# FFT convolution of one 224x224 image with a 7x7 kernel: the order of the first copies, and which pixel transforms precede the first round

## The chip, the cores and the metric

The kernel runs on one core of a Trainium2 chip. The core has five engines that run side by side: TensorE (PE, matrix products; its weight loads are listed as PEld), VectorE (DVE), ScalarE (ACT), GpSimd (POOL) and SyncE (SP), which here only issues DMA transfers. Data comes from HBM into SBUF (128 partitions); products land in PSUM (8 banks), from where VectorE or ScalarE evict them. The metric is the device time of one launch in microseconds, the median of several runs. Lower is better.

## The reference

A circular convolution over a 224x224 image with 96 input and 96 output channels, 7x7 taps, written as a product of spectra. Inputs are bfloat16, the spectra are float32, and the result is rounded to bfloat16.

```python
# x: (1, 224, 224, 96), w: (7, 7, 96, 96), both bfloat16
def reference(x, w):
    B, H, W, C = x.shape
    K = w.shape[0]
    wp = jnp.pad(w, ((0, H - K), (0, W - K), (0, 0), (0, 0)))
    Xf = jnp.fft.rfft2(x.astype(jnp.float32), axes=(1, 2))
    Wf = jnp.fft.rfft2(wp.astype(jnp.float32), axes=(0, 1))
    Yf = jnp.einsum('bhwi,hwio->bhwo', Xf, Wf)
    return jnp.fft.irfft2(Yf, s=(H, W), axes=(1, 2)).astype(jnp.bfloat16)
```

## The kernel before, in words

**What it computes.** Rows are transformed, columns are not. The 224 rows are cut into 8 blocks of 28 output rows; each block with its 6 rows of overlap is taken to 17 "slots" s = 0..16 by a matrix `Fm` (a DFT of length 32 and two extra real values). Slots 0 and 16 hold two real values each, the other 15 a complex one, which is multiplied with three real products (parts 0, 1, 2). Along a row the 7 taps are applied directly, on even and odd pixels apart, with 10 tap matrices per slot and part (`NTAP`, 7 taps and 3 sums). Per slot the channels are contracted on TensorE by matmuls of 96 columns with the transformed weights `WF` (`b_round`). The results `yf` go to a scratch in HBM, are loaded again, and a matrix `G` takes them back to rows.

**Tiles.** The image is worked in 7 tiles of 32 columns (t = 0..6). A tile's pixels come in two halves of 112 rows and 6 overlap rows (`jg` = 0, 1). Tile 0 lies in `x0_bufs`, tile 1 in `xn_bufs`; tile 0 also needs 6 columns from the right edge of the image, the halo (`xh_bufs`).

**Pixel transforms.** `f_jobs(t, part)` transforms the pixels of tile 0, 1 or 2 for a range of slots: `SH2 = (0, 8, 13, 17)` makes part 0 slots 0 to 7, part 1 slots 8 to 12, part 2 slots 13 to 16. A job is 8 or 16 matmuls (weights are one pixel column, moving data is `Fm`, 64, 40 or 32 columns wide for the three parts) into a PSUM bank, and one eviction to `xf`. Each part and half has 32 matmuls. The halo is done by `a_bank`. `jit(t, g)` then builds on VectorE the differences and sums `J` of a group of three slots, which the rounds read.

**Weights.** The 49 tap matrices of 96x96 lie with taps on partitions. A first copy stands on partitions 30 to 78 of `wqx` (`W1 = 30`), a second, shifted by 48 output channels, on 79 to 127. Each copy is one transfer of 48 rows (`load_w`) and two of the last row (`load_last`). The unused places of `wqx` are set to zero by ScalarE (`zero_a`) and one memset. `wide_jobs` (24 jobs of four matmuls, eviction to `WF`) makes the weights of slots 0 to 4 from the first copy alone. `prep_jobs(gi)` makes those of slots 5 to 16, in four groups of three slots, from both copies. `diff(s)` makes part 2 from parts 0 and 1.

**What sets the order.** Every engine runs its instructions in the order written: the class `_Ordered` (line 91) chains them. An eviction goes to VectorE or ScalarE by a running cost of each (`load`, line 132). All loads are issued by SP, one after the other; SP waits for an earlier transfer's landing when it needs that transfer's semaphore again. The head (lines 203 to 223) issues the loads and starts 14 dummy matmuls; GpSimd, VectorE and ScalarE build the factors `Em`, the transform `Fm` and the zero fills; `build_g` (line 339) computes `G` on GpSimd, with one Sin on ScalarE and a last product in `g_fin`. Then follow (lines 759 to 778) the pixel jobs of half 0, the wide jobs, with halo, half 1 of part 0 and `jit(0, 0)` among them, and dummy matmuls in between.

**Rounds.** After the head, tiles 0 and 1 run as one sequence of rounds r = 0..20 (line 819): tile 0 does slot r, and from r = 4 on tile 1 does slot r - 4. Each round has two places for other work, in mid round and at its end, numbered k = 2r and 2r + 1. `add(a, b, jobs)` spreads a list of jobs over the places a to b - 1; the lists run at each place in the order in which they were added, the `prep_jobs` ahead of the pixel jobs. The first group of `prep_jobs` begins at place 4, the middle of round 2. Tiles 2 to 6 follow, tile by tile.

Of the kernel before, what the change touches and what calls it, by code (L numbers as in the profile page):

```python
# [47 lines left out]
FILL = 3  # L48
FEV = 4
WMID = 14  # L50
JIT0 = 20
W1 = 30
ZA = 1000
# [13 lines left out]
def kernel(  # L67
# [134 lines left out]

    load_x(0, 0)
    load_last(K1 - 1, 0)
    load_w(W1, 0, PW - 1, 0)
# [33 lines left out]
    pi_t = ftile([128, 1])  # L239
    VE.memset(pi_t[:], math.pi)  # L240
    dmy = ftile([128, 1])
    SE.activation(out=dmy[:], in_=pi_t[:], func=ACTF.Sin, bias=0.0, scale=0.0)
# [7 lines left out]

    nrj = ftile([EP, JG]); pw_i = ftile([EP, 1]); aa = ftile([EP, NS, 2]); phf = ftile([EP, NS, 2]); phe = ftile([EP, NS, 2])
# [16 lines left out]
    VE.scalar_tensor_tensor(out=tap[:], in0=ha[:], scalar=-float(PW), in1=pw_i[:], op0=ALU.mult, op1=ALU.add)  # L268
    floor_div(VE, thp[:], tap[:], KT)
# [9 lines left out]
    SE.activation(out=qq[:], in_=qq[:], func=ACTF.Sin, bias=pi_t[:], scale=-2.0 * math.pi / Q)  # L279
    zero_a(W1, ZA, ZB)  # L280

    GE.memset(mf[:], 1.0)
# [10 lines left out]
    iota(twc[:], [[1, KT]])  # L293
    twp = ftile([EP, 1]); mk = ftile([EP, NTAP]); mk2 = ftile([EP, 2, NTAP])
    th7 = ftile([EP, 1])
    GE.tensor_single_scalar(out=th7[:], in_=thp[:], scalar=-float(KT), op=ALU.mult)
    GE.tensor_tensor(out=twp[:], in0=th7[:], in1=tap[:], op=ALU.add)
    GE.tensor_scalar(out=mk[:, 0:KT], in0=twc[:], scalar1=twp[:, 0:1], scalar2=None, op0=ALU.is_equal)
    GE.tensor_tensor(out=mk[:, KT:NTAP], in0=mk[:, 0:6:2], in1=mk[:, 1:6:2], op=ALU.add)
    VE.scalar_tensor_tensor(out=hm[:, 0:1], in0=hb[:], scalar=-2.0, in1=ha[:], op0=ALU.mult, op1=ALU.add)  # L300
    VE.scalar_tensor_tensor(out=hm[:, 1:2], in0=pw_i[:], scalar=float(PW), in1=hm[:, 0:1], op0=ALU.is_ge, op1=ALU.subtract)
    for h in range(2):
        GE.tensor_scalar(out=mk2[:, h], in0=mk[:], scalar1=hm[:, h:h + 1], scalar2=None, op0=ALU.mult)
    for xb in xh_bufs:
        GE.memset(xb[:, PAD * C:], 0.0)
    for xb in xn_bufs:
        GE.memset(xb[:, XW:], 0.0)

    VE.tensor_tensor(out=Fm.rearrange("p r s j -> p j s r"), in0=qq[0:R, 0:JG],
                     in1=mf.rearrange("p j (s r) -> p j s r", r=2), op=ALU.mult)  # L310
    qe = qq[:, JG]
    pe3 = ftile([EP, NSLOT])
    VE.memset(wz[0:W1, ZB:WE // 2], 0.0)
# [8 lines left out]
    def factors(h0, h1, out_ap, in_ap):  # L322
# [7 lines left out]
        else:  # L330
# [5 lines left out]
            pe3[:, 5:14].rearrange("p (s r) -> p s r", r=3)[:, :, 0:2])  # L336
    factors(0, 2, Em[:, :, NW0:], pe3[:, NW0:])
    factors(1, 2, Em[:, 1, 0:NW0], pe3[:, 0:NW0])

    def build_g(nj):  # L340
        PG = nj * FR

# [9 lines left out]
        p = ftile([PG, 1]); sp = ftile([PG, 1]); rm = ftile([PG, 1]); jp = ftile([PG, 1]); rr = ftile([PG, 1]); z = ftile([PG, 1])  # L352
        iota(p[:], [[0, 1]], cm=1)
        mod_g(rm[:], p[:], jp[:], FR)
        mod_g(rr[:], rm[:], sp[:], 2)
        GE.tensor_single_scalar(out=z[:], in_=sp[:], scalar=0.0, op=ALU.is_equal)
        zr = ftile([PG, 1]); ag = ftile([PG, 1]); pg = ftile([PG, 1]); amp = ftile([PG, 1]); pgt = ftile([PG, 1])
        GE.tensor_tensor(out=zr[:], in0=z[:], in1=rr[:], op=ALU.mult)
        GE.tensor_scalar(out=ag[:], in0=zr[:], scalar1=LC / 2.0, scalar2=sp[:, 0:1], op0=ALU.mult, op1=ALU.add)
        en = ftile([PG, 1]); ne = ftile([PG, 1]); tg = ftile([PG, 1])  # L360
        GE.tensor_single_scalar(out=en[:], in_=sp[:], scalar=NS - 1.0, op=ALU.is_equal)
        GE.tensor_scalar(out=ne[:], in0=en[:], scalar1=-1.0, scalar2=1.0, op0=ALU.mult, op1=ALU.add)
        GE.tensor_scalar(out=ag[:], in0=ag[:], scalar1=2.0, scalar2=ne[:, 0:1], op0=ALU.mult, op1=ALU.mult)
        GE.tensor_tensor(out=pgt[:], in0=rr[:], in1=zr[:], op=ALU.subtract)
        GE.tensor_tensor(out=pgt[:], in0=pgt[:], in1=ne[:], op=ALU.mult)
        GE.tensor_scalar(out=pg[:], in0=pgt[:], scalar1=LC / 2.0, scalar2=LC / 2.0, op0=ALU.mult, op1=ALU.add)
        GE.tensor_scalar(out=amp[:], in0=z[:], scalar1=-1.0 / LC, scalar2=2.0 / LC, op0=ALU.mult, op1=ALU.add)
        GE.tensor_tensor(out=amp[:], in0=amp[:], in1=ne[:], op=ALU.mult)
        GE.tensor_tensor(out=amp[:], in0=amp[:], in1=en[:], op=ALU.add)
        GE.tensor_scalar(out=tg[:], in0=rr[:], scalar1=B - 1.0, scalar2=PAD - 1.0, op0=ALU.mult, op1=ALU.add)  # L370
        GE.tensor_tensor(out=tg[:], in0=tg[:], in1=en[:], op=ALU.mult)
        GE.tensor_single_scalar(out=jp[:], in_=jp[:], scalar=2.0 * B, op=ALU.mult)
        GE.tensor_tensor(out=tg[:], in0=tg[:], in1=jp[:], op=ALU.add)
        nm = ftile([PG, nj, B]); jc = ftile([PG, nj, B]); msk = ftile([PG, nj, B]); fl = ftile([PG, nj, B]); th = ftile([PG, nj, B])
        iota(nm[:], [[0, nj], [1, B]], base=PAD - 1)
        iota(jc[:], [[2 * B, nj], [0, B]])
        GE.tensor_scalar(out=msk[:], in0=nm[:], scalar1=en[:, 0:1], scalar2=None, op0=ALU.mult)
        GE.tensor_tensor(out=msk[:], in0=msk[:], in1=jc[:], op=ALU.add)
        GE.tensor_scalar(out=msk[:], in0=msk[:], scalar1=tg[:, 0:1], scalar2=amp[:, 0:1], op0=ALU.is_equal, op1=ALU.mult)
        GE.tensor_scalar(out=nm[:], in0=nm[:], scalar1=ag[:, 0:1], scalar2=pg[:, 0:1], op0=ALU.mult, op1=ALU.add)  # L380
        mod_g(th[:], nm[:], fl[:], Q)

        def fin():
            SE.activation(out=th[:], in_=th[:], func=ACTF.Sin, bias=pi_t[0:PG, :], scale=-2.0 * math.pi / Q)
            GE.tensor_tensor(out=G.rearrange("p (j m) -> p j m", j=nj), in0=th[:], in1=msk[:], op=ALU.mult)
# [140 lines left out]
    def jit(t, g):  # L526
# [10 lines left out]
        def sub(o, a, b, op, cost):  # L537
            def f():
# [7 lines left out]
        dpl = bass.AP(x1.tensor, x1.offset - NJ, [pd, [NJ, 2], rd, sd, qd])  # L546
        return [
            sub(Jb[:, 0:4, 0:n].rearrange("c (k r) s q -> c k r s q", r=2), dpl,
                x0.unsqueeze(1).to_broadcast([C, 2, 2, n, PP]), ALU.subtract, 4 * PP * n),
# [211 lines left out]
    for p in range(3):  # L761
        for f in fj[p][0]:
            f()
    warm(FILL)
    for i, f in enumerate(wide_jobs()):
        if i == WMID:
            for jg in range(2):
                for g in a_bank(0, xf0, xh_bufs[jg], 0, 3, jg, 0):
                    g()
            for g in fj[0][1]:  # L770
                g()
        f()
        if i == JIT0:
            for g in jit(0, 0):
                g()
        if i % FEV == FEV - 1:
            warm(1)
    g_fin()
    stmp_cm.__exit__(None, None, None)
    yf_pool = ctx.enter_context(tc.tile_pool(name="yf", bufs=YBUF))  # L780
    tv_pool = ctx.enter_context(tc.tile_pool(name="tv", bufs=2))
# [193 lines left out]
```

## Time and profile before

| | us |
|---|---|
| median of 3 runs (lowest, highest) | 271.03 (269.06, 271.15) |
| the profiled execution | 269.31 |
| its span on the core | 267.5 |

| stretch of the span | length, us | PE busy, us | what runs on TensorE |
|---|---|---|---|
| 0 to 6.73 | 6.73 | 5.36 | 14 dummy matmuls |
| 6.73 to 10.67 | 3.94 | 3.34 | 96 pixel matmuls of half 0, 3 dummies |
| 10.67 to 20.73 | 10.06 | 9.12 | wide jobs, halo, half 1 of part 0, dummies |
| 20.73 to 27.20 | 6.47 | 5.13 | rounds 0, 1 and the start of 2 |
| 27.20 to 37.70 | 10.50 | 10.47 | rounds 2 to 4 |
| 37.70 to 60 | 22.30 | 21.52 | rounds |
| 60 to 230 | 170.00 | 168.83 | rounds and tiles 2 to 6 |
| 230 to 267.4 | 37.40 | 31.28 | last tile's end and output |

Times inside the span are counted from its start. Busy times are what the profile records; matmuls overlap, so the spacing of their starts tells what one costs. The rest of a run's time, 269.31 - 267.5 = 1.8 us, lies around the span.

### The profile page before, as it was taken

Reading aid. Unit: us, or ns where it says so; the run is one execution under the profiler, and the core shown is the slowest. Engines: PE = TensorE matmul, PEld = TensorE weight load, DVE = VectorE, ACT = ScalarE, POOL = GpSimd, SP = SyncE. Lnnn points to the kernel's source line nnn. Section 1 sums busy time; section 2 is a strip of 40 time slices with the busy share of each in tenths; the row PEclk is TensorE's granted clock in tenths of the full one; section 3 lists DMA queues with packets and bytes.
Section 4 is the critical chain, followed back from the end, with each engine's and each line's share of the span. In section 5 each row is a group of like instructions: output and inputs, shape, how many; then the busy total and the mean of one; then the engine's idle time right before and its main releaser. Section 6 shows DMA issues by size and latency. Waiting matters only on the chain. (4 is left out here: it accounts for less than half of the span.)

```text
span 267.5 us, 12139 instructions
## 1 busy us (share of the span) xinstructions
PE 255.1 (95%) x5128; PEld 235.7 (88%) x5128; DVE 216.2 (81%) x465; ACT 197.6 (74%) x485; POOL 97.7 (37%) x152
## 2 busy tenths in 40 slices
PE   8897999999999999999999999999999999999983
PEld 2787999999998999999999998989999889879861
DVE  7997699889899788778887888778888789978523
ACT  8796978497964578998988789886988864187123
POOL 7771324364558344222222322233123323422100
PEclk9999999999999999999999999999999999999998
DMA  8994102711111697987876486979678443887845
GB/s 197 230 251 76 48 2 67 245 45 48 47 48 49 192 258 159 294 238 223 272 195 188 117 235 221 253 216 341 235 152 242 169 128 125 204 250 182 259 107 191
DMA packets 46690, 46.78 MB, mean 175 GB/s; under 512 B 35292, under 2 KB 38056, under 8 KB 46540
## 3 DMA queue, kind: packets, MB, share of 16 engines
q1 hardware_dynamic: 44348, 43.95, 59.6%
q10 hardware_dynamic: 2288, 2.06, 2.6%
q8 instruction: 40, 0.66, 1.1%
q14 instruction: 14, 0.11, 0.2%
HBM read 24.66 MB, written 21.33 MB: 172 GB/s over the span
## 5 line engine op out<-in xcount | busy, mean ns | idle before, releaser
L101 PE MATMUL pb<-WF,J 96*128 96x96 bf16 x2821 | 162.9, 206 | 1.7 <-DVE J L101 1.3
L101 PEld LDWEIGHTS <-J 96*128 96x128 bf16 x2821 | 138.0, 98 | 12.3 <-issue 3.5
L101 POOL TENSOR_TENSOR yf<-v,u 128x384 bf16<-128x384 f32 x79 | 81.3, 1040 | 145.7 <-issue 84.6
L101 ACT CAST xf<-pb 96x408 bf16<-96x408 f32 (+3 forms) x145 | 67.3, 486 | 7.6 <-PE pb L101 3.8
L101 PE MATMUL pb<-WF,xf 96*128 96x96 bf16 x952 | 60.0, 206 | 0.9 <-ACT WF L101 0.9
L101 DVE TENSOR_TENSOR J<-xf 96x1824 bf16<-96x1824 bf16 (+1 forms) x84 | 56.9, 716 | 0.0
L101 PEld LDWEIGHTS <-xf 96*128 96x128 bf16 x952 | 47.2, 98 | 1.3 <-issue 1.2
L101 PE MATMUL pb<-Fm,xn 118*128 118x136 bf16 (+3 forms) x640 | 45.5, 199 | 0.2 <-DVE u L101 0.2
L101 PE MATMUL pb<-tt,Gm 102*84 102x384 bf16 (+1 forms) x132 | 32.9, 326 | 0.6 <-ACT J L101 0.3
L101 PEld LDWEIGHTS <-xn 118*128 118x128 bf16 x640 | 30.3, 97 | 0.3 <-issue 0.3
L101 ACT CAST WF<-pb 96x480 bf16<-96x480 f32 (+1 forms) x58 | 28.6, 558 | 2.3 <-PE pb L101 2.3
L101 ACT CAST J<-pb 84x384 bf16<-84x384 f32 (+1 forms) x65 | 28.1, 490 | 2.6 <-PE pb L101 2.6
L101 ACT CAST yo<-pb 84x384 bf16<-84x384 f32 (+1 forms) x63 | 27.1, 486 | 2.3 <-POOL yf L101 1.3
L101 DVE TENSOR_TENSOR J<-J 96x912 bf16<-96x912 bf16 (+2 forms) x42 | 24.2, 576 | 0.0
L101 PE MATMUL pb<-wq 128*128 128x120 bf16 (+1 forms) x288 | 21.8, 226 | 0.7 <-DMA wq<-in_w_dram 0.6
L101 PEld LDWEIGHTS <-wq 128*128 128x128 bf16 (+1 forms) x288 | 19.9, 148 | 1.7 <-DVE xf L101 1.1
L101 DVE TENSOR_TENSOR yf<-v,u 128x384 bf16<-128x384 f32 x26 | 15.1, 580 | 0.9
L101 PE MATMUL pb<-wu 128*112 128x384 bf16 (+1 forms) x59 | 14.5, 391 | 1.1 <-DVE ct L101 1.1
L101 PEld LDWEIGHTS <-wu 128*112 128x112 bf16 (+1 forms) x59 | 7.4, 127 | 5.6 <-issue 3.1
L101 PEld LDWEIGHTS <-Gm 102*84 102x84 bf16 (+1 forms) x132 | 11.1, 117 | 1.0 <-issue 0.4
L101 ACT COPY xf<-xf 96x816 bf16<-96x816 bf16 (+3 forms) x20 | 11.1, 613 | 0.0
L101 ACT CAST tt<-pb 112x384 bf16<-112x384 f32 x8 | 3.6, 480 | 9.3 <-PE pb L101 9.2
(387 smaller groups left out, 239.2 us busy)
## 6 DMA issues: line engine op xcount, KB each, us to landing
scr<-yf SPq DMA_DIRECT2D x30, 288.0 KB
xn<-in_x_dram SPq DMA_DIRECT2D x12, 672.0 KB
tt<-scr SPq DMA_DIRECT2D x24, 336.0 KB
out_dram<-yo SPq DMA_DIRECT2D x12, 252.0 KB
out_dram<-J SPq DMA_DIRECT2D x12, 252.0 KB
tt<-scr SPq DMA_DIRECT2D x6, 288.0 KB
WF<-in_x_dram SPq DMA_DIRECT2D x2, 672.0 KB
out_dram<-tt SPq DMA_DIRECT2D x8, 168.0 KB
```

The costliest lines, as they stand in the source:

```text
L101: r = fn(*a, **k)
```

## The change

- **Loads.** The first weight copy is issued first, then its last row, then the pixels of tile 0's first half. Everything behind stays.
- **Head order.** No pixel job runs ahead of the wide jobs. Four dummies lead them (`FILL` 4 for 3). Half 0 of part 0 runs ahead of wide job 12 (`WX0`), the halo ahead of job 18 (`WHALO`), half 1 of part 0 behind the last wide job, then two dummies and `jit(0, 0)`. `load["v"]` is raised by 900 before the wide jobs.
- **Parts 1 and 2 of tile 0** run wholly in the rounds: part 1 at the places 1 to 5, part 2 at 6 to 9. Before, half 0 of both was in the head, half 1 at the places 1 to 3 and 3 to 6.
- **`jit`.** The first group's first operation is cut in two, slot 0 and slots 1, 2.
- **Rounds.** `diff(2..4)` comes one place later; the copy of tile 0's last columns to tile 1 for part 0 comes in round 2 instead of 1; `g_fin` in round 3 instead of at the end of the head.
- **Set-up.** The dummy Sin follows the first two zero fills. The limits of the fills change (`ZA` 1200 for 1000). The memset of the rest goes from VectorE to GpSimd. GpSimd makes the tap masks `mk2` before the mask `mf`; VectorE makes the first two factors before `Fm`. `build_g` and `pi_t` use the buffer `J_bufs[2]` instead of tiles of their own.

```diff
-FILL = 3
+FILL = 4
 FEV = 4
-WMID = 14
-JIT0 = 20
+WX0 = 12
+WHALO = 18
 W1 = 30
-ZA = 1000
+ZA = 1200
...
+    load_w(W1, 0, PW - 1, 0)
+    load_last(K1 - 1, 0)
     load_x(0, 0)
-    load_last(K1 - 1, 0)
-    load_w(W1, 0, PW - 1, 0)
...
-    pi_t = ftile([128, 1])
-    VE.memset(pi_t[:], math.pi)
-    dmy = ftile([128, 1])
-    SE.activation(out=dmy[:], in_=pi_t[:], func=ACTF.Sin, bias=0.0, scale=0.0)
+    J2f = J_bufs[2].bitcast(F32)
+    pi_t = J2f[:, 0:1]
+    VE.memset(pi_t, math.pi)
...
     zero_a(W1, 0, ZA)
+    dmy = ftile([128, 1])
+    SE.activation(out=dmy[:], in_=pi_t, func=ACTF.Sin, bias=0.0, scale=0.0)
...
     zero_a(W1, ZA, ZB)
+    iota(twc[:], [[1, KT]])
...
+        GE.tensor_scalar(out=mk2[:, h], in0=mk[:], scalar1=hm[:, h:h + 1], scalar2=None, op0=ALU.mult)
+    GE.memset(wz[0:W1, ZB:WE // 2], 0.0)
...
-    VE.memset(wz[0:W1, ZB:WE // 2], 0.0)
...
     factors(0, 1, Em[:, 0, 5:NW0].rearrange("p (s r) t -> p s r t", r=2),
             pe3[:, 5:14].rearrange("p (s r) -> p s r", r=3)[:, :, 0:2])
+    VE.tensor_tensor(out=Fm.rearrange("p r s j -> p j s r"), in0=qq[0:R, 0:JG],
+                     in1=mf.rearrange("p j (s r) -> p j s r", r=2), op=ALU.mult)
...
+        cuts = ((0, 1), (1, n)) if t == g == 0 else ((0, n),)
         return [
-            sub(Jb[:, 0:4, 0:n].rearrange("c (k r) s q -> c k r s q", r=2), dpl,
-                x0.unsqueeze(1).to_broadcast([C, 2, 2, n, PP]), ALU.subtract, 4 * PP * n),
+            sub(Jb[:, 0:4, a:b].rearrange("c (k r) s q -> c k r s q", r=2), dpl[:, :, :, a:b],
+                x0[:, :, a:b].unsqueeze(1).to_broadcast([C, 2, 2, b - a, PP]), ALU.subtract, 4 * PP * (b - a)) for a, b in cuts] + [
...
-    for p in range(3):
-        for f in fj[p][0]:
-            f()
     warm(FILL)
+    load["v"] += 900
     for i, f in enumerate(wide_jobs()):
-        if i == WMID:
+        if i == WX0:
+            for g in fj[0][0]:
+                g()
+        if i == WHALO:
             for jg in range(2):
                 for g in a_bank(0, xf0, xh_bufs[jg], 0, 3, jg, 0):
                     g()
-            for g in fj[0][1]:
-                g()
         f()
-        if i == JIT0:
-            for g in jit(0, 0):
-                g()
         if i % FEV == FEV - 1:
             warm(1)
-    g_fin()
+    for g in fj[0][1]:
+        g()
+    warm(2)
+    for g in jit(0, 0):
+        g()
...
-                add(2 * i - 4, 2 * i - 3, [diff(i)])
-            add(1, 4, fj[1][1])
-            add(3, 7, fj[2][1])
+                add(2 * i - 3, 2 * i - 2, [diff(i)])
+            add(1, 6, fj[1][0] + fj[1][1])
+            add(6, 10, fj[2][0] + fj[2][1])
+        if r == 2:
+            new_xf(1, SH2[0], SH2[1])
...
+        if r == 3:
+            g_fin()
```

## The prediction

> **What bounds the kernel now.** I read the busy table first, then the stretches, then the head in order of time.
>
> ```profile
> PE 255.1 (95%) x5128; PEld 235.7 (88%) x5128; DVE 216.2 (81%) x465; ACT 197.6 (74%) x485; POOL 97.7 (37%) x152
> ```
>
> TensorE is the bound on average. The view of stretches shows where it is not (columns: stretch, its length, busy us and instructions of PE, PEld, DVE, ACT, POOL, then granted clock, DMA share, GB/s):
>
> ```profile
> 0.00:6.73 6.73, 5.36 (x14) 1.85 (x14) 4.97 (x28) 5.81 (x6) 5.15 (x33) 1.00 0.81 195
> ...
> 10.67:20.73 10.06, 9.12 (x146) 8.47 (x147) 9.48 (x18) 8.98 (x20) 7.06 (x26) 1.00 1.13 260
> 20.73:27.20 6.47, 5.13 (x138) 4.91 (x138) 4.10 (x8) 4.40 (x12) 1.16 (x2) 1.00 0.30 49
> 27.20:37.70 10.50, 10.47 (x266) 10.50 (x267) 8.89 (x16) 10.23 (x27) 2.96 (x3) 1.00 0.09 32
> ...
> 60.00:230.00 170.00, 168.83 (x3541) 160.04 (x3538) 142.68 (x302) 133.47 (x340) 61.25 (x62) 1.00 0.66 186
> ```
>
> From 27.20 on TensorE is full: 0.03 us idle in 10.5, 1.17 us in 170. So a matmul moved behind 27.2 costs its full time, and only what opens that full stretch earlier can bring anything. Before it, TensorE stands still several times (timelines of PE and of its weight loads, PEld; columns: start, length, work, count, idle before it and who ended it):
>
> ```profile
> 10.70 1.19 PE L101 MATMUL pb<-wq 79*128 79x128 bf16 x16 [0.60 <-DMA wq<-in_w_dram]
> ...
> 20.73 0.50 PE L101 MATMUL pb<-WF,xf 96*128 96x96 bf16 x8 [0.91 <-ACT WF L101]
> ...
> 25.30 0.50 PE L101 MATMUL pb<-Fm,WF 118*128 118x32 bf16 x14 [1.23 <-issue]
> ...
> 27.20 0.81 PEld L101 LDWEIGHTS <-wq 128*128 128x128 bf16 x12 [0.25 <-DMA wq<-in_w_dram]
> ```
>
> The first is the wait for the first weight copy that the change attacks. The last is the one that decides here: `wq` on 128 rows means the first `prep_jobs` matmul of round 2, which reads both weight copies, and it waits for the second. So the full stretch opens when the second copy has landed, and round 2 reaches that point just in time now.
>
> **The second copy hardly moves.** The view of one-microsecond stretches shows it. SP issues the same 18 transfers; only the order of the first five differs.
>
> ```profile
> 20.00:21.00 1.00, 0.27 (x7) 0.27 (x7) 1.00 (x4) 0.94 (x3) 0.00 (x0) 1.00 1.57 226
> ...
> 22.00:23.00 1.00, 1.00 (x33) 1.00 (x30) 0.52 (x1) 0.94 (x3) 0.00 (x0) 1.00 0.46 62
> ...
> 24.00:25.00 1.00, 0.08 (x4) 0.00 (x0) 1.00 (x3) 0.57 (x2) 0.00 (x0) 1.00 0.18 48
> 25.00:26.00 1.00, 0.69 (x26) 0.69 (x26) 1.00 (x2) 0.16 (x1) 0.00 (x0) 1.00 0.03 5
> ```
>
> The DMA share is full until about 21 and then runs down over 5 us: a few engines are late, the others done. The trace's landing records give the second copy's last piece at 27.1. Every engine has the same bytes to move in the new order. What can change is idle time: between the first pixels' last packet (about 3.9) and the first weight packet (4.17) lie some 0.25 us that a large copy in front would close. SP's waits for landings stay: now the 13th issue waits until 10.59 for the weights' landing, the next ones for the halo rows; in the new order the pixels land second and are waited for instead, and the halo rows' landing (10.9 to 11.5) holds the second copy's issue at about 11.7 either way. I take -0.25 us, bounds -2.6 (all engines as early as the median one, whose last piece lands near 24.5) and +0.7 (one more 18 KB packet-time on a late engine).
>
> **The head before that point.** Added: ScalarE's built order now has two table loads, since a copy comes ahead of the first Sin; now there is one.
>
> ```profile
> 0.80 1.28 ACT L101 ACT_TABLE_LOAD   x1 [0.80 <-PEq L959]
> ...
> 2.20 1.96 ACT L101 COPY wq<-wu 128x1036 f32<-128x1036 f32 x2
> ...
> 4.61 2.34 ACT L101 COPY wq<-wu 30x2600 f32<-30x2600 f32 x1
> ```
>
> New sum on ScalarE: load to 2.08; two fills of 1036 and 1200 columns, 1.96+0.18, to 4.2; second load 1.28 to 5.5; dummy 0.20 and Sin 0.44 to 6.1; fill of 2400 columns, 2.34x2400/2600 = 2.16, to 8.3. The Trainium skill ("ScalarE: Activation LUTs", What ACT_TABLE_LOAD costs) adds a drain of about 1.38 us to each 1.28 us load. By that the fill would end near 9.7; the trace shows the next ACTIVATE 0.01 us after the load and no drain. The first wide matmul waits for this fill, for the weights (885 KB from 1.8 us; at the 200 to 390 GB/s of 3 to 7 us they land between 5.5 and 7.5) and for the factors on VectorE (Sin 6.1, then 0.6 of small operations and 0.4 for two factors: 7.1). So wide work starts at 8.4, not when the weights land: 2.3 us earlier than 10.70.
>
> Until round 0 TensorE then has 96 wide matmuls with warm ones (1.21 us per 16: 7.3), 64 pixel matmuls of 64 columns (29 ns each: 1.9) and 12 halo ones (0.7): 9.9, to 18.3. The evictions are as long: ScalarE 14 x 0.48 + 4 x 0.45 + 2 x 0.46 = 9.4 from 8.9, VectorE as much from 9.4 (Fm and the later factors, 0.77 and 1.2, now stand behind the first factors), to 18.8. Round 0 can start near 19.1; its differences J are no longer built beside wide work, but only the first slice (608 elements, 0.46) is ahead of it. Rounds 0 and 1 take 0.9+0.4 and 0.8+0.4+0.6+0.7 us of matmuls, with about 0.3 for J and 19 matmuls of round 2 (0.8): the `prep_jobs` matmul is reached near 24, against 26.9 now. That is 3 us earlier than its data. The 1.4 us stop at 23.9 in mid-group ("issue", beside a 16 KB instruction fetch that waited in the loaded queue) may recur, and is covered by the same 3 us; so are the table load and POOL's added fill (1008 columns; on VectorE 0.90 us), which all count nothing while that cover lasts. `g_fin` moved to round 3 frees 0.38 on ScalarE here. Its product (0.78 on POOL) then stands ahead of a round's sum, where POOL idles 2 to 5 us each time. `build_g` now lives in the buffer of tile 1's first J, so that J (1.2 on VectorE, in round 3, with an eviction and round 4's u queued behind it) waits for this product; by order it is done about 2 us before, so I cost the wait at nothing, at most 0.8.
>
> **What is left behind 27.** Groups by form give pixel matmuls of 40 and 32 columns; in the timeline 16 of them take 0.40 us, 25 ns each. Of these 128, all but 16 are done by 27.2 now. In the new order round 0 has 16 and round 1 has 24 of them before the wait, so 88 remain, 72 more. They stand behind the waiting `prep_jobs` matmul in TensorE's queue and cannot fill its 3 us. Cost: 72 x 25 ns = **+1.8 us**, none of it hidden, by the 10.47 of 10.50 above.
>
> Their evictions are 3 of 320 and 3 of 512 elements: 3 x 0.36 + 3 x 0.5 by spacing = 2.6 us, plus the Sin of `g_fin`, 0.3. ScalarE has 0.27 us free in 27.2 to 37.7, VectorE 1.61, and each gains 1.8 by the longer stretch: 2.9 into 5.5, so it fits. But u of every round waits for ScalarE's scaling, which stands behind evictions in that queue, and a late u holds banks. Bounds: 0 if well interleaved; +1.4 if all 2.9 must be ScalarE's (2.9+0.6 of halo copies, less 2.1 free). I take +0.3, nearer the fit. Later slack can give some back (0.78 idle us in 37.7 to 60): 0 to 0.5, I take 0.2.
>
> **Sum.** -0.25 + 1.8 + 0.3 - 0.2 = +1.65 us. The profiled execution took 269.31 (span 267.5 and 1.8 around it), so 271.0 by its own level. The median of the runs, 271.03, lies 1.7 above that, so I forecast 271.03 + 1.6 = **272.6**: slower by 0.6%, within the 1% that about separates a change from none here.
>
> **Rivals.**
> - *The head's gain comes through (not slower).* The second copy's stragglers come at 24.5: then -2.6 + 1.8 + 0.3 - 0.2 = -0.7 us, 270.3. For: the tail is only a few engines (share 0.18 at 24). Against: same bytes, same issue times. Even without any wait, 2.3 us of earlier start is the ceiling, so faster by over 1% (2.7 us) needs luck in level as well.
> - *ScalarE becomes the bound in rounds 2 to 5 (slower by over 1%).* Place: the scaling of rounds 3 and 4 behind five to six evictions, halo copies and the moved Sin. Price: the upper bound 1.4 in place of 0.3, +2.75 in all, 273.8. It decides once the added ScalarE work exceeds 2.1 us. For: ScalarE 10.23 of 10.50, and u waits 1.0 to 1.5 us for it in rounds 1 to 3 already. Against: VectorE's free 1.6.
> - *The long wait slows TensorE's clock.* The opening matmuls of 512 columns came every 0.43 us, later ones at 0.21, so TensorE starts at half pace for about 4 us. If an idle time of 3 us brings that back, 4 us at half pace lose 2 us: +3.65, 274.7. Against: 1.41 us idle at 23.9 did not, and any stop on the way shortens the wait. The Trainium skill ("TensorE: Matmul & The Clock Gate", Why this matters for your kernels) asks for no idle gaps above about 3 us; the trace's longest here is below that and shows full clock.
> - *The change doesn't do what it says*: if the wide work still began near 10.7 (fills or factors late), `prep_jobs` would be reached at 26.3, still under cover: the same 272.6.
>
> **Chances.** Forecast, with the fourth rival, 0.62; gain comes through 0.14; ScalarE 0.16; clock 0.08. Range: from the first rival on the lower level of the runs, 269.6, to the third, 274.6. Over 1% slower: the clock's 0.08, two thirds of ScalarE's 0.16 and a tenth of the rest, 0.26; faster only by level, 0.04; within 0.70.
>
> **What would show it.** Right: first wide matmul near 8.4; round 0 near 19; TensorE idle for 2 to 3 us before the first `wq` load on 128 rows, ended by DMA, near 27; 40- and 32-column pixel matmuls after it. Wrong: that load before 25.5, or round 5 starting no later than in the kernel before.

## The result

| | median, us | lowest to highest, us | runs |
|---|---|---|---|
| kernel before, beside the changed one | 269.47 | 267.80 to 271.15 | 22 |
| changed kernel | 271.05 | 269.70 to 273.14 | 22 |

Changed over before: **1.0059** with a 95% interval of 1.0037 to 1.0082, so 1.6 us slower. The forecast was slower by 0.6%, "within 1%" the likeliest, and the sum came out: +1.65 against +1.58 us. Several of its terms did not; errors of opposite sign cancel in it, so the close agreement is luck. The time of 272.6 us lies 1.55 above the measured one (the range held it), since it stood on 271.03, the median of three runs of the kernel before, which is 269.47 over the 22 runs here. Ratios here and below leave out runs more than 1.5% above the fastest of the same kernel, so they are not always the quotient of the two medians. The profiled execution of the changed kernel has a span of 269.3 us, 1.8 more than before.

### The profile page after: what moved, and what is told of

Its sections match the earlier page's. It is cut to its first block, busy times and chain, and to the rows that moved or that the text cites. A ratio compares the mean times of both kernels' runs of the same rounds, so it can differ in the third digit from the quotient of the medians.

```text
span 269.3 us, 12143 instructions
## 1 busy us (share of the span) xinstructions
PE 257.2 (96%) x5131; PEld 237.3 (88%) x5131; DVE 216.5 (80%) x465; ACT 198.2 (74%) x486; POOL 99.1 (37%) x153
## 5 line engine op out<-in xcount | busy, mean ns | idle before, releaser
L101 DVE TENSOR_TENSOR J<-xf 96x456 bf16<-96x456 bf16 (+3 forms) x85 | 56.9, 709 | 0.1
L101 PE MATMUL pb<-wu 128*112 128x384 bf16 (+1 forms) x62 | 15.3, 395 | 1.0 <-DVE J L101 1.0
L101 DVE TENSOR_TENSOR WF<-WF 96x960 bf16<-96x960 bf16 x14 | 10.3, 772 | 0.0
```

The lines of the kernel that those rows point to most:

```text
L101: r = fn(*a, **k)
```

## The profile after

Busy times of the changed kernel, from its page:

```profile
PE 257.2 (96%) x5131; PEld 237.3 (88%) x5131; DVE 216.5 (80%) x465; ACT 198.2 (74%) x486; POOL 99.1 (37%) x153
```

TensorE works 2.1 us longer than before with the same products and three matmuls more. Work that has not grown but takes longer is a matter of pace. Stretches of the changed kernel (columns as before: stretch, length, busy us of PE, PEld, DVE, ACT, POOL, granted clock, DMA share, GB/s):

```profile
7.10:9.59 2.49, 0.38 (x3) 0.04 (x1) 2.01 (x5) 1.05 (x1) 2.16 (x14) 1.00 0.98 259
9.59:20.06 10.47, 10.45 (x181) 9.38 (x181) 8.80 (x16) 9.39 (x20) 8.22 (x33) 1.00 1.07 254
20.06:27.75 7.69, 6.39 (x131) 6.14 (x131) 5.12 (x10) 3.19 (x9) 1.11 (x2) 0.78 0.39 76
...
62.30:232.30 170.00, 168.85 (x3542) 160.06 (x3539) 142.53 (x301) 133.76 (x341) 61.26 (x62) 1.00 0.66 186
```

The long middle stretch is the one from before, 2.3 us later: the same 168.8 us of 170. All of the loss arises in the first 45 us. There, 20.06 to 27.75 stands out with a granted clock of 0.78. The same time in single microseconds:

```profile
22.00:23.00 1.00, 0.40 (x15) 0.40 (x15) 0.63 (x3) 0.00 (x0) 0.00 (x0) 0.97 0.44 79
23.00:24.00 1.00, 1.00 (x20) 1.00 (x17) 1.00 (x2) 0.75 (x2) 0.00 (x0) 0.50 0.42 91
24.00:25.00 1.00, 1.00 (x23) 1.00 (x21) 0.03 (x1) 0.20 (x1) 0.00 (x0) 0.50 0.09 23
25.00:26.00 1.00, 1.00 (x21) 1.00 (x19) 0.36 (x1) 0.85 (x3) 0.00 (x0) 0.50 0.04 12
26.00:27.00 1.00, 1.00 (x32) 1.00 (x30) 0.55 (x2) 0.33 (x2) 0.00 (x0) 0.82 0.00 0
```

TensorE is busy throughout, but starts 20 to 23 matmuls per microsecond (before, in 22 to 23: 33). The shortfall from full clock adds up to 3.42 us at half speed. The 58 matmuls that begin in it take 3.46 us; the same 58 take 2.13 and 2.19 us in two profiles below whose clock held (`e6` and `e7`), so 1.3 us are lost. The timeline of PE in the changed kernel gives what came ahead of it (start, length, work, count, idle before and who ended it):

```profile
9.59 1.18 PE L101 MATMUL pb<-wq 79*128 79x128 bf16 x16 [2.11 <-POOL J L101]
...
20.06 0.52 PE L101 MATMUL pb<-WF,xf 96*128 96x96 bf16 x8
21.11 0.73 PE L101 MATMUL pb<-WF,J 96*128 96x96 bf16 x13 [0.54 <-DVE J L101]
22.60 0.20 PE L101 MATMUL pb<-WF,J 96*128 96x96 bf16 x1 [0.76 <-issue]
...
27.75 0.94 PE L101 MATMUL pb<-wq 128*128 128x120 bf16 x12
```

Against before (10.70, 20.73 and 27.20 for the first, second and last line): the wide work starts 1.1 us earlier, round 0 starts 0.7 us earlier, and the first `prep_jobs` matmul 0.5 us **later**, waiting for nothing. The second copy's last piece landed at 26.66, 1.1 us ahead of it. So the idle time of 2 to 3 us that I forecast there is not in this trace.

Why the wide work began at 9.59 and not at 8.4: the timelines of ScalarE and of VectorE in the changed kernel.

```profile
4.25 1.28 ACT L101 ACT_TABLE_LOAD   x1
5.54 0.20 ACT L101 ACTIVATE ct<-J 128x1 f32<-128x1 f32 x1
...
5.98 2.17 ACT L101 COPY wq<-wu 30x2400 f32<-30x2400 f32 x1
```

```profile
7.51 0.76 DVE L101 TENSOR_TENSOR Fm<-ct,ct 118x136 bf16<-118x136 f32 x1 [0.23 <-POOL ct L101]
7.89 1.48 DVE L101 TENSOR_TENSOR wq<-ct,ct 128x780 bf16<-128x780 f32 x2
```

The second of these lines merges two operations. The view of the tile `wq` (shortest, median and longest duration in ns; first and last start; shapes) has the last one, of 110 columns, start at 9.1:

```profile
L101 DVE TENSOR_TENSOR wq<-ct,ct x4: 210/244/1175, 6.9 to 9.1; 128x50 bf16<-128x50 f32 x1, 128x60 bf16<-128x60 f32 x1, 128x780 bf16<-128x780 f32 x1, 128x110 bf16<-128x110 f32 x1
```

ScalarE's fill ended at 8.15 (forecast 8.3): both table loads are there, and the next ACTIVATE follows 0.01 us after the second. The Trainium skill's drain ("ScalarE: Activation LUTs", What ACT_TABLE_LOAD costs) does not show, and the 9.7 us that I worked out from it, with one drain, does not occur. What was late is VectorE. A wide matmul reads 128 factor columns; the first two factor operations write 110 of them, and the other 18 come from the operation of 780 columns, behind `Fm`, which ended at 9.07. TensorE did not start then: in the trace its wait for VectorE ended at 9.42, right behind the operation of 110 columns (9.10 to 9.38), although by the code that one writes columns that no wide matmul reads. So the start hangs on all four factor operations. The wait's label, POOL, is not what ended it: POOL's work on `J` in this stretch began only at 7.88, and no wide matmul reads it.

## The experiments

Times stand beside runs of the kernel before on the same chip: its median was 269.22 (20 runs) for the first four, 269.44 (15) for the next four, 269.23 (29) for the last four.

### One part alone in the kernel before

`e1`: only half 0 of parts 1 and 2 goes to the rounds.

```diff
-    for p in range(3):
-        for f in fj[p][0]:
-            f()
+    for f in fj[0][0]:
+        f()
...
-            add(1, 4, fj[1][1])
-            add(3, 7, fj[2][1])
+            add(1, 6, fj[1][0] + fj[1][1])
+            add(6, 10, fj[2][0] + fj[2][1])
```

> The kernel before with one part of the change alone: half 0 of parts 1 and 2 of tile 0 leaves the head and runs in the rounds, at the changed kernel's places. Loads, head and set-up stay as before. Theory 'moved work' (the prediction's): the first weight matmul of round 2 still comes near 27.2, ended by the second copy, and 72 more pixel matmuls stand behind it in a full stretch: +1.6 to +1.8 us, ratio near 1.006. Rival 'clock' (the change's cost is the half clock that the trace of the changed kernel shows from 22.6 to 26.2 us, 0.50 granted): with the head of before the clock stays at 1.00 and the cost is 0 to +0.4 us.

Measured: 272.32 us (268.58 to 275.16, 12 runs), ratio 1.0077 [1.0038, 1.0117]. The profile, of an execution of 274.08 us, shows that this does not measure the moved work. PE's timeline, and stretches of one microsecond:

```profile
10.76 1.86 PE L101 MATMUL pb<-wq 79*128 79x128 bf16 x16 [2.81 <-DMA wq<-in_w_dram]
```

```profile
10.00:11.00 1.00, 0.24 (x3) 0.27 (x4) 0.00 (x0) 0.00 (x0) 0.72 (x4) 0.93 1.09 280
11.00:12.00 1.00, 1.00 (x13) 1.00 (x11) 0.19 (x1) 0.52 (x1) 0.74 (x5) 0.50 1.02 270
...
20.00:21.00 1.00, 1.00 (x24) 1.00 (x22) 0.83 (x2) 0.64 (x2) 0.00 (x0) 0.50 1.37 269
21.00:22.00 1.00, 1.00 (x19) 0.92 (x17) 0.80 (x2) 0.73 (x3) 0.00 (x0) 0.95 0.86 131
```

Where the moved matmuls had been, TensorE now waited 3 us for the first weights, and then ran at half clock for 10 us. It is not this execution alone: nine of the 12 runs have a mean clock of 0.987 or less. So the experiment was repeated with dummies in the hole.

`e9`: `e1`, and

```diff
-FILL = 3
+FILL = 15
```

> The kernel before with only the half 0 of parts 1 and 2 moved into the rounds, as in the first experiment, and with 15 dummy matmuls in the place of 3 ahead of the wide work, to bridge the 3.18 us in which TensorE idled there and after which its clock dropped. Theory (the 72 moved matmuls are owed behind the landing of the second copy, and cost what they take, 1.3 to 1.8 us, if the clock holds): more than half of the runs at a mean clock of 0.998 or more, TensorE waiting for the second copy near 27 us, and a median 1.2 to 1.8 us above the kernel before. Rival (the moved work is free, and the first experiment's 3 us were all clock): a median within 0.5 us of the kernel before.

Measured: 269.35 us (268.53 to 272.01, 12 runs), ratio 1.0020 [0.9991, 1.0049], so -0.2 to +1.3 us. Twelve dummies, which compute nothing, gained 3 us against `e1` by the medians, 1.5 us by the ratios. The rival's time holds, and the clock did (1.00 in every microsecond from 5 to 45). But the moved work was not free, as the rival has it. PEld's timeline shows a wait:

```profile
25.67 0.81 PEld L101 LDWEIGHTS <-wq 128*128 128x128 bf16 x12 [0.28 <-DMA wq<-in_w_dram]
```

The second copy landed at 25.61 in this execution, and the first matmul followed 0.09 us later, 1.5 us earlier than in the kernel before (27.23). The moved matmuls are owed behind it, and the two cancel. With this landing the kernel before could not have gained as much, since TensorE itself gets there at 26.9: its second copy holds it back only in runs where it lands behind 26.9, and in how many it does was not measured.

### One part taken back from the changed kernel

`e2`: half 0 of parts 1 and 2 returns to the head, ahead of wide job 12.

```diff
-            for g in fj[0][0]:
+            for g in fj[0][0] + fj[1][0] + fj[2][0]:
                 g()
...
-            add(1, 6, fj[1][0] + fj[1][1])
-            add(6, 10, fj[2][0] + fj[2][1])
+            add(1, 4, fj[1][1])
+            add(3, 7, fj[2][1])
```

> The changed kernel with that part undone: half 0 of parts 1 and 2 runs in the head, ahead of wide job 12 with part 0, and half 1 has its old places. Theory 'moved work': round 0 starts some 1.5 to 2 us later than in the changed kernel (64 matmuls, six evictions on two engines), the rest behind 27 is 1.8 us shorter, so -0.5 to +0.3 us against the kernel before, about 1.5 faster than the changed one. Rival 'clock': if the gaps around round 0 bring the half clock again, +1 to +2 us against before, as the changed kernel.

Measured: 273.54 us (272.52 to 273.94, 6 runs), ratio 1.0157 [1.0121, 1.0192]. Taking the part back made the kernel slower still, by 2.5 us; the expectation missed. PE's timeline:

```profile
18.92 0.74 PE L101 MATMUL pb<-wq 79*128 79x128 bf16 x9
22.60 0.85 PE L101 MATMUL pb<-wq 79*128 79x128 bf16 x7 [2.94 <-issue]
```

TensorE stops in the middle of the wide work for an instruction fetch, and then has half clock for 3.42 us. In the trace 448 instructions of TensorE's queue stand ahead of the stop, as many as ahead of the one at 22.60 in the changed kernel; with 64 more matmuls and their weight loads in the head, that point is reached earlier (19.43), ahead of the fetch of 16 KB at 19.59 to 20.91. So the experiment does not tell the price of the moved part. It shows that in this head undoing the move costs more than it saves.

`e3`: the load order of before.

```diff
-    load_w(W1, 0, PW - 1, 0)
-    load_last(K1 - 1, 0)
     load_x(0, 0)
+    load_last(K1 - 1, 0)
+    load_w(W1, 0, PW - 1, 0)
```

> The changed kernel with the three load lines back in the order of before (pixels, last row, weight copy). Theory of the prediction (3 us of cover ahead of the second copy): wide work starts near 10.7 instead of 9.6 and nothing else changes: as the changed kernel, +1.6 us against before. Rival 'head start' (round 2 is reached after its data, 27.5 against a landing of 26.7 in the trace, so each us of the head counts): +2.7 us against before, 1.1 above the changed kernel.

Measured: 272.61 us (270.88 to 274.16, 6 runs), ratio 1.0130 [1.0085, 1.0175]. The first wide matmul came at 10.11 instead of 9.59, after 2.8 us of idle time; the clock was halved for 10.24 us, and the first `prep_jobs` matmul came at 30.19. The two runs without a drop took 270.88 and 271.34. Nothing here shows that the new load order loses time; how much of the difference is the clock, six runs do not tell.

### The clock

`e4` and `e6` add dummies and no work: `e4` two more ahead of `jit(0, 0)` and three in round 0, `e6` ten more ahead of the wide work.

```diff
 e4
             SE.copy(out=tt_[:, 0:2 * C], in_=b0[:, 0:2 * C])
+            if t == 0 and s == 0:
+                warm(3)
             mid()
...
-    warm(2)
+    warm(4)
     for g in jit(0, 0):
 e6
-FILL = 4
+FILL = 14
```

> The changed kernel with five more dummy matmuls: two behind the head's two, three in round 0 between the matmuls on the pixels and those on J, where TensorE waits 0.40 and 0.75 us. Theory 'clock': the granted clock stays 1.00 through 20 to 27, round 1 takes some 1.4 us less, round 2's first weight matmul waits for the second copy near 26.8 instead of coming at 27.75: 0.9 us faster than the changed kernel, +0.7 against before; all of +1.6 gone if the clock is the whole cost. Theory 'moved work' alone: with the clock up or not, no more than 0.9 us comes back, since the 72 matmuls stay behind the landing.

> The changed kernel with 14 dummy matmuls in the place of 4 ahead of the wide work, so that they end near 9.3 us and the idle stretch of 2.5 us from 7.1 to 9.6 us is gone; no work of the kernel differs. Theory (the clock drops after idle stretches, and this one is a cause): the share of runs with a mean granted clock of 0.998 or more rises from 7 of 22 to over two thirds, and the median comes to that of the changed kernel's full-clock runs, 270.4 us, 0.7 us below its 271.05. Rival (the gaps around round 0, at 19.65 to 22.6 us, decide alone): the profile still shows a granted clock of 0.5 at 23 to 26 us, and the median stays within 0.3 us of the changed kernel's.

Measured: `e4` 271.12 us (269.65 to 272.73, 9 runs), ratio 1.0080 [1.0051, 1.0110]; `e6` 272.25 us (270.45 to 272.66, 6 runs), ratio 1.0099 [1.0065, 1.0132]. A mean clock of 0.998 or more was found in 6 of 9 and 2 of 6 runs, against 7 of 22 of the changed kernel; the medians of these runs are 270.9, 271.0 and 270.4. The share rose with `e4` alone, and in time neither gained. The 270.4 expected of `e6` missed, and its rival's drop at 23 to 26 us did not come either: the profiled execution of `e6` had no drop at all and still took 271.45. In `e4`'s the clock held from 20 to 27 us, as expected, but had been halved from 11.6 to 15.0, behind the idle stretch ahead of the wide work, and the first `prep_jobs` matmul came at 28.11, waiting for nothing. PE's timeline of `e6`:

```profile
27.50 0.92 PE L101 MATMUL pb<-wq 128*128 128x120 bf16 x12 [1.80 <-DMA wq<-in_w_dram]
```

This is the wait of the prediction: TensorE ready at 25.5, two microseconds idle, ended by the second copy, which landed at 27.42. In this execution, where the clock held, that copy was the bound.

### The late factors

`e7`: `Fm` goes behind the factor operations. `e10`: `e7`, and `FILL` 11.

```diff
-    VE.tensor_tensor(out=Fm.rearrange("p r s j -> p j s r"), in0=qq[0:R, 0:JG],
-                     in1=mf.rearrange("p j (s r) -> p j s r", r=2), op=ALU.mult)
     factors(0, 2, Em[:, :, NW0:], pe3[:, NW0:])
     factors(1, 2, Em[:, 1, 0:NW0], pe3[:, 0:NW0])
+    VE.tensor_tensor(out=Fm.rearrange("p r s j -> p j s r"), in0=qq[0:R, 0:JG],
+                     in1=mf.rearrange("p j (s r) -> p j s r", r=2), op=ALU.mult)
```

> The changed kernel with the 0.76 us operation on Fm moved behind the two large factor operations of VectorE. Theory (the first wide matmul waits for the 128x780 factor operation that wrote its last 18 columns, not for the weights or for POOL): that matmul starts 0.7 to 1.1 us earlier, at 8.5 to 8.9 us, and round 0 near 19.0 to 19.4 us; of that up to 1.1 us reaches the end if nothing takes the place of the wait, and the median falls by 0.3 to 1.1 us. Rival (another input sets the start, the zeroing by ScalarE that ended at 8.15 us or the copy that landed at 8.1 us): it stays at 9.3 us or later. Second rival: it starts earlier, and TensorE gives the gain back at the second copy or at an instruction fetch: round 0 earlier, the first load on 128 rows at the same time, the median within 0.3 us.

> The changed kernel with Fm behind the factors and 11 dummies in the place of 4, so that TensorE has no idle stretch ahead of the wide work; the load order is that of the changed kernel. Theory (with the clock held, the second copy's landing sets the time): TensorE comes to the first weight load on 128 rows at 25.0 us or before, waits there for the copy (26.0 to 27.4 us), and the time after that load is 241.1 to 242 us of span as in the two runs before it; so a median of 269.0 to 270.6 us, and runs that differ by what the copy's landing differs. Rival (the clock is lost elsewhere, at the instruction fetch near 20 us): the profile shows a granted clock of 0.5 after 20 us, and the median stays at 271 us or more.

Measured: `e7` 271.90 us (269.04 to 273.09, 6 runs), ratio 1.0103 [1.0067, 1.0139]; `e10` 272.43 us (269.68 to 273.63, 6 runs), ratio 1.0112 [1.0067, 1.0157]. The mechanism of the late start is shown: in `e7` the last factor operation ends at 8.46, and the first wide matmul follows at 8.66 instead of 9.59, 0.2 us behind that operation as in the changed kernel; round 0 comes at 19.12. So the expected cause holds, but for which of the two large operations ends the wait, and the expected gain does not: the time did not fall (the intervals of its ratio and the changed kernel's overlap). What took the place of the wait in the profiled execution, the fastest of the six, is again the copy. PEld's timeline of `e7`:

```profile
26.05 0.81 PEld L101 LDWEIGHTS <-wq 128*128 128x128 bf16 x12 [1.41 <-DMA wq<-in_w_dram]
```

In `e10` the copy landed at 27.55, and the wait was the longest of all. PE's timeline, and the microseconds behind it:

```profile
27.64 0.96 PE L101 MATMUL pb<-wq 128*128 128x120 bf16 x12 [2.77 <-DMA wq<-in_w_dram]
```

```profile
29.00:30.00 1.00, 1.00 (x26) 1.00 (x23) 1.00 (x3) 0.95 (x3) 0.00 (x0) 0.68 0.06 16
30.00:31.00 1.00, 1.00 (x15) 1.00 (x13) 0.67 (x2) 0.00 (x0) 0.00 (x0) 0.50 0.00 0
31.00:32.00 1.00, 1.00 (x19) 1.00 (x18) 1.00 (x3) 0.98 (x3) 0.75 (x1) 0.50 0.00 0
32.00:33.00 1.00, 1.00 (x25) 1.00 (x22) 1.00 (x1) 1.00 (x4) 0.57 (x1) 0.61 0.00 0
```

That is the prediction's third rival: a wait of 3 us for the second copy, and then half clock for 3.42 us, in the stretch that has no idle time to absorb it. Its price is 1.4 us (the 50 matmuls that begin in it take 3.40 us, and 2.0 in `e6` and `e7`), where the rival had 2. What was expected of `e10` holds up to the copy (TensorE ready at 24.7); behind it, the span left is 243.2 us instead of 241.1 to 242, and the median lies 1.8 us above the expected range. Both signs of its rival came, half clock after 20 us and a median above 271, but the clock falls at the copy's wait, not at the fetch, where the rival had it.

### The second copy earlier

`e5`: the second copy ahead of both halves of tile 1. `e8`: the same with `e7`'s edit and `FILL` 10. `e11`: `e10` with the copy ahead of the second half only. `e12`: `e11` without the dummies inside the wide work (`FEV` 1000).

```diff
 e5, e8
+    load_w(K1, 0, PW - 1, 1)
+    load_last(EP - 1, 1)
     for jg in range(2):
         load_x(1, jg)
-    load_w(K1, 0, PW - 1, 1)
-    load_last(EP - 1, 1)
 e11, e12
-    for jg in range(2):
-        load_x(1, jg)
+    load_x(1, 0)
     load_w(K1, 0, PW - 1, 1)
     load_last(EP - 1, 1)
+    load_x(1, 1)
```

> The changed kernel with the second weight copy issued ahead of both halves of the second tile's pixels; nothing else differs. Theory of the prediction (the end of the head is set by the second copy, which landed at 26.66 us): the copy now lands 4 to 6 us earlier, TensorE comes to its first weight load on 128 rows up to 1.8 us earlier than in the changed kernel, and the median falls by 1.0 to 1.8 us, to the level of the kernel before. Rival (nothing waits for that copy, since the late start of the wide work, the gaps around round 0 and the half clock have used up the slack before it): the load on 128 rows stays within 0.5 us of 27.75 where the clock drops as before, and the median lies within 0.5 us of the changed kernel's (ratio to the kernel before 1.004 to 1.008). A second rival: the second tile's pixels, now 2 us later, hold back round 1, and the time rises by 0.5 to 2 us.

> The changed kernel with all three edits: Fm behind the factors, the second weight copy ahead of both halves of the second tile's pixels, and 10 dummy matmuls in the place of 4 ahead of the wide work. If the late factors, the half clock and the copy are each a part of what the change lost, their sum shows here: wide work from 8.6 us, the first load on 128 rows at 24.4 to 26 us, and 72 matmuls of 1.8 us still owed behind it, so a median 0.0 to 1.0 us below that of the kernel before. If the moved matmuls alone make the difference, and the rest is hidden, it stays 1.3 to 1.8 us above the kernel before.

> As the run before it in this list, and the second weight copy issued ahead of the second half of the second tile's pixels. Theory (the copy's landing sets the time as long as the clock holds): the copy lands 2 to 3 us earlier, near 24 us, the load on 128 rows follows at 24.3 to 25.2 us, and the median falls by 0.8 to 1.8 us against the run before it in this list, to or below the kernel before (268 to 269.4 us). Rival (TensorE's own work and the fetch stop reach that load no earlier): no difference above 0.4 us.

> As the run before it in this list, without the six dummy matmuls inside the wide work (0.21 us each). Theory (TensorE is the bound in the wide work, where its idle time is below 0.1 us, and the copy lands early enough): the wide work ends up to 1.3 us earlier, the instruction block's end is reached 12 instructions later, and the median falls by 0.3 to 1.2 us against the run before it. Rival (the evictions of VectorE and ScalarE, busy 3.8 of 4 us, set the pace, or the fetch does): TensorE idles in their place, the time is the same within 0.3 us, or the clock drops and it is 1 us or more slower.

| | median, us | lowest to highest | runs | ratio to before |
|---|---|---|---|---|
| `e5` | 273.24 | 270.70 to 275.01 | 6 | 1.0129 [1.0088, 1.0171] |
| `e8` | 270.80 | 269.77 to 271.99 | 10 | 1.0060 [1.0037, 1.0084] |
| `e11` | 271.47 | 268.99 to 272.19 | 12 | 1.0075 [1.0045, 1.0106] |
| `e12` | 270.80 | 269.26 to 273.33 | 12 | 1.0060 [1.0029, 1.0090] |

No profile of these four has a wait for the second copy any more, and none is faster than the kernel before. `e5` was 2.2 us above the changed kernel by the medians, 1.9 by the ratios, the size of its second rival, but what the profile shows is another loss: TensorE idled 3.4 us ahead of the wide work, 0.9 more than in the changed kernel, and had half clock for 6.84 us; the load on 128 rows came at 29.42. Its one run above 0.998 took 270.70. In the other three the instruction fetch stopped TensorE at the same count of its recorded instructions as in the changed kernel, for 1.5, 0.7 and 2.1 us by the spacing of matmuls, and half clock followed for 3.40 us each time. PE's timeline of `e12`:

```profile
22.43 0.22 PE L101 MATMUL pb<-WF,J 96*128 96x96 bf16 x1 [1.94 <-issue]
```

So with the copy out of the way the fetch and the clock are next, and they take what it gave. `e8` came where its rival had it, 1.4 us above the kernel before, but its profile has this stop and half clock beside the moved matmuls. `e11` and `e12` fell below the one before them in the list by 1.0 and 0.7 us, which are the expected sizes, though the intervals of the ratios overlap, their load on 128 rows came at 26.6 and 27.6 instead of 25, and `e11` missed the 268 to 269.4 us that it was to reach. No edit here beats the kernel before; `e9` cannot be told from it.

### All profiles side by side

P is the start of the first `prep_jobs` matmul on 128 rows. The lag is how much later than in the kernel before the same matmul runs, counted from the end (the 4,301st, at 45.3 us there); from there to 202 us it changes by less than 0.15 us in every row. The last column is the lag less P's own delay, lag - (P - 27.23): what is owed behind P. Each row is one execution, which need not stand for the median: `e7`'s is 2.9 us below its median and `e11`'s 1.6, `e1`'s 1.8 above.

| | second copy landed | P | P waits for the copy | half clock, us | lag | owed |
|---|---|---|---|---|---|---|
| before | 27.14 | 27.23 | yes, 0.3 | none | 0 | |
| `e9` | 25.61 | 25.70 | yes, 0.3 | none | -0.13 | 1.40 |
| `e7` | 25.99 | 26.08 | yes, 1.4 | none | 0.19 | 1.34 |
| `e6` | 27.42 | 27.50 | yes, 1.9 | none | 1.67 | 1.40 |
| `e10` | 27.55 | 27.64 | yes, 2.9 | 3.42, behind P | 3.07 | 2.66 |
| changed | 26.66 | 27.75 | no | 3.42 | 2.30 | 1.78 |
| `e11` | 24.63 | 26.61 | no | 3.40 | 0.90 | 1.52 |
| `e8` | 22.17 | 27.18 | no | 3.40 | 1.77 | 1.82 |
| `e12` | 25.24 | 27.61 | no | 3.40 | 1.78 | 1.40 |
| `e4` | 26.69 | 28.11 | no | 3.40 | 2.69 | 1.81 |
| `e5` | 22.29 | 29.42 | no | 6.84 | 3.99 | 1.80 |
| `e1` | 26.78 | 29.89 | no | 10.24 | 4.30 | 1.64 |
| `e3` | 25.13 | 30.19 | no | 10.24 | 4.73 | 1.77 |
| `e2` (nothing moved) | 26.43 | 31.31 | no | 3.42 | 5.00 | 0.92 |

In all five rows with a wait, P follows the landing by 0.08 to 0.09 us. In three of them the clock held, and the owed work agrees to 0.06 us. From P to the 4,301st matmul from the end the traces have 430 matmuls in the kernel before and in `e2`, and 502 in every other: the 72 of the prediction. What `e2` owes without them are stops of TensorE (the longest, from 35.2 us on, are of 0.31, 0.49 and 0.46 us), so "owed" holds stops as well as work.

## Why the prediction was right, and where it was not

**The price behind the second copy: right in kind, a little too high.** 72 matmuls at 25 ns, +1.8, +0.3 for evictions, -0.2 of later slack: 1.9. Measured: 1.34 to 1.40 where the clock held, 1.78 in the changed kernel's own profile. The count of 72 is in the traces, and the 1.8 itself fits. The slack was mis-sized: the kernel before stands still for 0.28 and 0.44 us at 40.2 and 41.9 us, `e7` for only 0.27 in all there, so 0.45 is given back, and 1.8 - 0.45 is 1.35. The evictions' 0.3 does not show in these profiles; in the changed kernel two stops of 0.27 and 0.33 us, at 29.4 and 33.9, are about its size.

**"The full stretch opens when the second copy has landed": right for that one profile, not for every run.** Before, TensorE was ready at 26.9 and the copy landed at 27.14; I read that as a bound. Landings in the ten profiles that leave it last lie between 25.1 and 27.6; with the load order of before, one in four lies behind 26.9. With an early landing the kernel before is bound by TensorE at 26.9, and work taken out of the head then brings P forward. `e9`'s profile shows this (P 1.5 us earlier, 1.40 owed, a lag of -0.13), and it would explain its median, 0.1 us above (-0.2 to +1.3 by the ratio), where the sum without its first term is 1.9; other landings in its other runs were not seen. The step that failed is the one that let a single profile's margin of 0.3 us decide.

**The -0.25 itself is not shown.** The copy landed at 26.66 against 27.14 here. But over the profiles, the old load order gives 27.14, 26.78, 25.61 and 25.13, the new one 25.99, 26.43, 26.66, 26.69, 27.42 and 27.55: if anything later. Ten numbers with a spread of 2.4 us don't settle it.

**The cover of 3 us: wrong.** The step "factors on VectorE: 7.1", and so "wide work starts at 8.4", failed: I counted the two operations that moved forward and missed that the matmul's 128 columns take in 18 of a third, and that the wait lasts until the fourth. That cost 1.2 us. Then round 0 began at 20.06 instead of 19.1 and lost 0.75 us for J and 0.96 us at the fetch (by the spacing of starts), and the half clock 1.3. So P came at 27.75 with the copy 1.1 us ahead of it, and -0.25 became +0.5. In the profile, +0.5 and 1.8 are the lag of 2.3, of which 0.5 came back by the end (spans of 269.3 and 267.5). The fourth rival stood on the same cover. Of the four signs that I gave for being right only the last came: 88 matmuls of 40 and 32 columns behind P, 16 in the kernel before.

**The clock: the rival had the kind of loss, too high a price, and the wrong place.** It was given 0.08, and 2 us, for a wait at the second copy. In the changed kernel it came behind three stops, none as long as 1 us, and cost 1.3; at the second copy it came in `e10`, and cost 1.4. The profiles without a drop in the work have a mean clock of 0.995 to 0.999, since idle time after the last work counts too. A run's mean clock of 0.995 or more was found in 49 of 64 runs of the kernel before (those beside the experiments; median 268.90) and in 10 of 22 of the changed one (270.30); below it, the medians are 270.40 and 271.41. So at equal clock the change costs 1.0 to 1.4 us, and the drops, 31 points more frequent and 1.1 us dear, add about 0.35.

**ScalarE as the bound** does not appear: in `e7` and `e9` TensorE is busy for 12.42 of 12.42 and 11.30 of 11.30 us behind P. **The gain comes through** was near in `e7`'s and `e9`'s profiles only, with copies at 26.0 and 25.6.

So the sum of +1.65 met +1.58 by errors of opposite sign, as far as these runs show: the moved part, which alone cost 0.1 us in `e9` by the medians, was priced at its full time, and a head that stops more often than before was taken to be covered. The late factors, the fetch and the clock are each shown in a profile, but their shares in the median are not separated: `e6` and `e7` took away one each, and the median did not fall. Why the changed kernel, at equal clock, is still about 1 us above `e9` (270.30 to 269.27) stays open; a later landing of the second copy in the new order would fit, and was not shown. A hint is that at a mean clock of 0.998 or more the kernels with an earlier second copy (`e5`, `e8`, `e11`, `e12`) have a median of 269.9 us in six runs, and those with it last (the changed kernel, `e4`, `e6`, `e7`, `e10`) one of 270.7 in 17; but they differ in other edits and in the chip.

## What to carry to other kernels

Ahead of a full stretch, ask in how many runs its opening is really bound by the transfer that one profile names: a margin of 0.3 us beside a landing that scatters by 2 us says little, and work moved out of the head and behind it can cost little in one run and its full time in another. When work is taken out of a stretch before a wait, the hole can itself be a cost, since TensorE's clock was halved behind such holes here (`e1`, `e3`, `e5`); fill it or measure it with dummies before judging the move. And list every operation that a matmul's start waits for, in the trace too, not only those whose results the plan has in mind.

## What was not expected of the hardware

- **The clock falls in periods.** Half clock lasted 3.40, 3.40, 3.40, 3.40, 3.42, 3.42, 3.42, 6.84, 10.24 and 10.24 us: one, two or three times 3.41. The Trainium skill ("TensorE: Matmul & The Clock Gate", What's actually happening) states a free-running window of 3413 ns, and the trace agrees: in each of the ten profiles with a drop in the work, its start and that of the drop behind the last work lie a whole number of 3.413 us apart (22.95 and 268.71 in the changed kernel, 72 of them), so the periods do not begin with the kernel's gaps. What it takes is less than the idle gap of about 3 us that the same page (Why this matters for your kernels) warns of: in the 3.41 us ahead of the drop TensorE had idled, by the spacing of its starts, 2.0 us in the changed kernel, 1.7 in `e10` and 1.6 in `e11`, in one to three pieces. And it need not follow. `e6` idled 2.0 us from 25.5 on with no drop behind it: counted back from its last drop, a period ended at 26.71 and parted this wait into 1.2 and 0.8 us. But the changed kernel stood still for 2.2 us, from 7.10 on, in the period that ended at 9.29, with no drop either, so idle time in the period is not all that decides; what else does stays open.
- **An instruction fetch can stop TensorE for 0.7 to 3.2 us.** Its fetches of 16 KB are in the trace. Where the first one behind 10 us was issued by 18.4 us (`e6`, `e7`, `e9`, `e10`), nothing stopped at the count of 448; where it was issued at 18.9 to 23.0, while the input copies filled the queues (`e2`, `e4`, `e5`, `e8`, `e12`, the changed kernel), TensorE stopped there; in `e1` and `e3` it came to that count only at 26. `e11`, issued at 18.2 and done at 19.6, stopped for 0.7 us at 20.5 all the same. The landing fits this: in all seven, TensorE went on 1.3 to 1.8 us after the fetch's last packet, while `e6`, `e7` and `e10` came to the count 1.7 to 1.9 us after it and `e9` 3.5. What decides the time of issue was not tried.
